# Attention heads in consecutive groups of four, tokens split by parity, and kT and qT written by VectorE's block transposes from the third group on

## The chip, the cores and the metric

The kernel runs on one core of one Trainium2 chip. The metric is device time in microseconds (us). The five engines are TensorE (PE in the profile; its weight loads are the row PEld), VectorE (DVE), ScalarE (ACT), GpSimd (POOL) and SyncE (SP). SP does no arithmetic here: it issues nearly all DMAs, in the order in which they stand in its queue.

## The reference, cut to what matters

```python
def sm_attn(qq, kk, vv):                       # softmax(qq kk^T / 8) vv
    s = scale * np.matmul(qq, kk.transpose(0, 1, 3, 2))
    a = np.exp(s - np.max(s, axis=-1, keepdims=True))
    return np.matmul(a / (np.sum(a, axis=-1, keepdims=True) + 1e-09), vv)
# q, k, v: 4 batches x 8 heads x 576 tokens x 64;  p: 4 x 8 x 32 x 64
p_packed = sm_attn(p, k, v)                    # 32 packed rows a head
x = sm_attn(q, p_packed, p_packed)             # 2304 tokens x 512 (8 heads side by side)
w = domain_probs / domain_probs.sum(-1)        # 2304 x 4
y = sum(w[:, e:e+1] * (np.maximum(x @ w1[e], 0) @ w2[e]) for e in range(4))   # 512 -> 1024 -> 512
h = y @ w_in                                   # 512 -> 2048
out = ((a0 + a1 h + a2 h^2 + a3 h^3) / (1 + |b0||h| + |b1|h^2)) @ w_out       # 2048 -> 512
```

## The kernel before

The attention is worked in eight groups of four heads (32 heads in all; two groups, x and y, for each batch bb). A group holds 4 x 32 packed rows on the 128 partitions. For each group k and q must stand with the head dimension on the partitions (tiles kT and qT: 128 partitions, 4 heads, 288 columns; partitions 0 to 63 hold one half of the tokens and 64 to 127 the other half). Both are loaded with tokens on 96 partitions, and TensorE turns them: `st_tr(i, nm, j)` (L293) makes six transposes for two heads into PSUM, and ScalarE copies them out (L294). So a group takes four calls of st_tr, two for k and two for q.

The rest of a group runs through short steps. `st_s1` multiplies p by kT (tile s), VectorE takes the maximum (mx), ScalarE the exponential (tile e). `st_e1t` transposes e on TensorE. `st_pp` multiplies by v (tile pp), VectorE scales it (ppd). `st_ppt` transposes that (tile bd). `st_s2` multiplies q by it, and VectorE transposes the scores in blocks of 32 x 32 (tile t). `st_m2`, `st_e2` and `st_a2` are the second softmax on VectorE, GpSimd and ScalarE. `st_at` turns it back in blocks, and `st_sp` splits it into a high and a low part (tiles aH and aL). `st_wb` and `st_wbl` fold the packed rows into the expert weight (tile wb).

Groups 0 and 1 run ahead of everything (the prologue, the first 28 us). The other six run between the units of the mixture of experts: 256 units (e, bb, half, c), numbered kk, each with six products into h (`emit_h`, L549), relu and split on ScalarE and VectorE (hh, hl) and, two units later, twelve products into acc (`emit_out`, L617). After them come 96 units of the last layer, with more columns each. The order in time is written out by hand: `at_step(kk, w, f, ...)` puts a step into unit kk, at w = 0 behind its h products and at w = 1 behind its acc products. The table of batch bb starts at unit s0 = (bb-1)*13 + 3 - bb//3, that is at 3, 16 and 28. All engines take their instructions in the program's order, so a waiting instruction holds back those behind it on its engine. All attention steps between the units share one PSUM buffer of two banks (`bank2`).

A group's tiles for k, q and v have one buffer each. The load of the next group is issued when the last transpose (or, for v, the last product) has read it. `store` writes rows of the output; its rows come in the token order that the loads made.

## Time and profile before

| what | value |
|---|---|
| time, median of 3 runs | 1133.42 us (1131.04 to 1133.48) |
| the profiled execution: its own time | 1133.6 us |
| its span, first to last instruction | 1131.8 us |
| PE busy | 1111.0 us, 98% |
| PEld busy | 1021.8 us, 90% |
| DVE / ACT / POOL busy | 718.9 / 522.2 / 314.0 us |
| granted TensorE clock, mean | 0.993 of full speed |
| moved by DMA | 125.93 MB |

The program stands in four stages: the prologue to 28 us, the units that have attention steps between them to some 180 us, the other units of the experts to some 700 us, and the last layer. Busy shares over the whole span mix these stages, so each is read by itself. A busy PE counts as busy while its products are in the pipeline; how far its weight loads (PEld) follow each other without a gap shows better whether it waits.

### The profile page before, as it was taken

The numbers are of one execution on the slowest core, as the hardware profiler recorded it, in microseconds if no ns is written. First come the engines' busy times: TensorE is split into PE (matmuls) and PEld (weight loads), VectorE is DVE, ScalarE is ACT, GpSimd is POOL, SyncE is SP. The second block draws the span as 40 slices with busy tenths as digits, with TensorE's granted clock in tenths as the row PEclk, the third lists the DMA queues.
The fourth block names the chain that finished last, engine by engine and source line by source line (L and its number), as shares of the span: only waits on it lengthen the run. The fifth ranks groups of instructions, "written<-read, shape, count | busy, mean of one in ns | idle before, by whom it ended". The sixth has DMA issues, their size and how long they took to land.

```text
span 1131.8 us, 20514 instructions
## 1 busy us (share of the span) xinstructions
PE 1111.0 (98%) x8145; PEld 1021.8 (90%) x8145; DVE 718.9 (64%) x1381; ACT 522.2 (46%) x1055; POOL 314.0 (28%) x315
## 2 busy tenths in 40 slices
PE   8899999999999999999999999999999999999997
PEld 6678788999999999999999999989999999999996
DVE  3343535727777746676442332599988888888885
ACT  4433433232222332222323221467778777787774
POOL 0511211132323343222433211253432222222222
PEclk9899999999999999999999999999999999999999
DMA  9542323332345233345310000533333634344421
GB/s 261 132 127 69 79 60 137 118 104 94 109 140 171 94 106 101 115 144 160 108 30 6 9 9 6 172 114 126 129 132 112 201 115 137 128 157 149 138 94 56
DMA packets 61920, 125.93 MB, mean 111 GB/s; under 512 B 6960, under 2 KB 29488, under 8 KB 61824
## 3 DMA queue, kind: packets, MB, share of 16 engines
q1 hardware_dynamic: 61504, 123.79, 35.5%
q8 instruction: 64, 1.05, 0.4%
q0 software_dynamic: 320, 0.82, 0.3%
q14 instruction: 32, 0.26, 0.1%
HBM read 103.06 MB, written 21.53 MB: 110 GB/s over the span
## 4 chain that ended last, share of the span: by engine, by line
PE 94%; DVE 2%; ACT 2%; POOL 1%; issue 1%; DMA 0%; POOLq 0%; ACTq 0%; DVEq 0%
PE acc L617 52%; PE h L549 36%; PE wb L147 3%; PE tr L293 1%; PE s L302 1%; PE e1t L327 1%; PE pp L339 0%; POOL t L378 0%; ACT e L315 0%; DVE mm L387 0%; DVE mx L310 0%; PE pT L274 0%; ACT hh L557 0%; PE pT L251 0%; DVE hl L558 0%
## 5 line engine op out<-in xcount | busy, mean ns | idle before, releaser
L617 PE MATMUL acc<-hh,w 128*128 128x288 f32 x2048 | 449.8, 296 | 0.0
L617 PEld LDWEIGHTS acc<-hh,w 128*128 128x128 f32 x2048 | 340.9, 188 | 8.8 <-issue 6.3
L558 DVE SCALAR_TENSOR_TENSOR hl<-h,hh 128x288 fp32r<-128x288 f32 x256 | 116.8, 456 | 294.0 <-ACT hh L557 293.5
L617 PE MATMUL acc<-hl,w 128*128 128x288 f32 x1024 | 300.8, 294 | 0.0
L557 ACT ACTIVATE hh<-h 128x288 fp32r<-128x288 f32 x256 | 104.9, 410 | 337.7 <-PE h L549 322.0
L549 PE MATMUL h<-aH,wb 128*128 128x288 f32 x1024 | 216.3, 300 | 2.2 <-ACT aH L405 2.2
L549 PE MATMUL h<-xH,w 128*128 128x384 f32 x768 | 196.2, 337 | 0.0
L617 PE MATMUL acc<-w,hh 128*128 128x512 f32 x576 | 193.1, 392 | 2.0 <-ACT s L563 2.0
L617 PEld LDWEIGHTS acc<-hl,w 128*128 128x128 f32 x1024 | 192.6, 188 | 0.0
L549 PEld LDWEIGHTS h<-aH,wb 128*128 128x128 f32 x1024 | 163.0, 188 | 28.6 <-issue 17.8
L594 POOL TENSOR_TENSOR hl<-c,hh 128x384 fp32r<-128x384 f32 x94 | 96.3, 1025 | 264.1 <-ACT hh L593 137.6
L549 PE MATMUL h<-aL,wb 128*128 128x288 f32 x512 | 151.3, 295 | 1.6 <-POOL aL L406 1.6
L549 PEld LDWEIGHTS h<-xH,w 128*128 128x128 f32 x768 | 140.1, 188 | 7.0
L549 PE MATMUL h<-xL,w 128*128 128x384 f32 x384 | 129.0, 336 | 0.0
L617 PEld LDWEIGHTS acc<-w,hh 128*128 128x128 f32 x576 | 108.8, 189 | 21.8 <-ACT s L563 2.3
L674 POOL TENSOR_TENSOR acc<-add,acc 128x288 f32<-128x288 f32 x96 | 75.9, 823 | 140.5 <-DVE add L672 140.5
L617 PE MATMUL acc<-w,hl 128*128 128x512 f32 x288 | 112.6, 391 | 0.0
L561 ACT ACTIVATE c<-h,small 128x384 f32<-128x384 f32 x96 | 64.7, 674 | 88.7 <-PE h L549 87.9
L549 PEld LDWEIGHTS h<-aL,wb 128*128 128x128 f32 x512 | 96.5, 188 | 2.4 <-POOL aL L406 2.4
L212 POOL TENSOR_TENSOR t<-u,raw 128x512 fp32r<-128x512 f32 x32 | 41.4, 1294 | 187.3 <-ACT raw L211 187.3
L567 DVE SCALAR_TENSOR_TENSOR m<-s,small,m 128x384 f32<-128x384 f32 x96 | 59.8, 623 | 47.9 <-ACT s L563 43.3
L549 PEld LDWEIGHTS h<-xL,w 128*128 128x128 f32 x384 | 72.2, 188 | 0.0
(111 smaller groups left out, 1291.9 us busy)
## 6 DMA issues: line engine op xcount, KB each, us to landing
w<-nw SPq DMA_DIRECT2D x96, 512.0 KB, 4.3
r<-in_moe_w_dram SPq DMA_DIRECT2D x32, 256.0 KB, 2.7
raw<-in_moe_w_in_dram SPq DMA_DIRECT2D x16, 512.0 KB, 4.3
raw<-in_moe_w_out_dram SPq DMA_DIRECT2D x16, 512.0 KB, 3.7
nw<-raw SPq DMA_DIRECT2D x32, 256.0 KB, 2.3
nw<-t SPq DMA_DIRECT2D x32, 256.0 KB, 2.6
r<-in_moe_w_dram SPq DMA_DIRECT2D x7, 1024.0 KB, 6.1
pw<-prow SPq DMA_DIRECT2D x32, 144.0 KB, 3.3
```

What stands on the lines that cost most here:

```text
L147: nc.tensor.matmul(ps[32 * c:32 * c + 32, g, :], bd[r, 2 * bb + g, 32 * c:32 * c + 32], raw1[fh][r, c, f], start=True, stop=True, tile_pos ...
L212: nc.gpsimd.tensor_tensor(out=wl, in0=f32(u), in1=f32(wh), op=ALU.subtract)
L293: nc.tensor.transpose(ps[:, hh, c * KP:c * KP + KP], src[2 * j + hh][:, c * 2 * D:(c + 1) * 2 * D], ident[:KP, :KP])
L302: nc.tensor.matmul(ps[32 * c:32 * c + 32, par, :HALF], w[r, 32 * c:32 * c + 32], xT[r, c, :], start=True, stop=True, tile_position=(64 * p ...
L549: nc.tensor.matmul(ps[:, :n], w, x, start=(i == 0), stop=(i == len(ops) - 1))
L557: nc.scalar.activation(out=hh, in_=ph, func=AF.Relu)
L558: nc.vector.scalar_tensor_tensor(out=hl, in0=ph, scalar=0.0, in1=f32(hh), op0=ALU.max, op1=ALU.subtract)
L561: nc.scalar.activation(out=c, in_=ph, func=AF.Identity, scale=a_sb[:, 3:4], bias=a_sb[:, 2:3])
L567: nc.vector.scalar_tensor_tensor(out=o, in0=x, scalar=scalar, in1=y, op0=op0, op1=op1, **kw)
L594: low.tensor_tensor(out=hl, in0=c, in1=f32(hh), op=ALU.subtract)
L617: nc.tensor.matmul(ps[:, :n], w, x, start=(first and i == 0), stop=(last and i == 2))
L674: nc.gpsimd.tensor_tensor(out=dst, in0=add, in1=dst, op=ALU.add)
```

## The change

Groups are heads 0 to 3 and 4 to 7 of a batch (before: even and odd heads). The two halves of the tokens are now the even and the odd tokens (before: by a token's place in runs of six).

Groups 0 and 1 keep their transposes on TensorE. Their loads and all loads of v have runs of 512 bytes (before 1536), so three times as many. The load of the probabilities has runs of 32 bytes (before 96). Each load of w1 is cut into two with 64 partitions each.

Groups 2 to 7 get k and q by `st_rows`: four DMAs for each tile, with 32 partitions each and runs of 128 bytes, laid out so that 32 x 32 block transposes on VectorE (`st_turn`, one for each head) give kT and qT directly. The 24 calls of st_tr for these groups and their copies on ScalarE are gone, and 48 calls of st_turn are there.

In the hand-written table the turns of k stand at s0 - 1 to s0 for group x and at s0 + 3 to s0 + 5 for group y, those of q behind s1. For x, s1 and e1t move half a unit later, m2, a2 half a unit earlier. For y, e1t moves one unit later.

```diff
-            nc.sync.dma_start(out=pn, in_=probs.rearrange("(b p c) e -> p b c e", p=KP, c=NKC))
+            nc.sync.dma_start(out=pn.rearrange("p b (j a) e -> p (b j) (a e)", a=2), in_=probs.rearrange("(b j p a) e -> p (b j) (a e)", b=B, p=KP, a=2))
...
-            nc.sync.dma_start(out=raw1[fh][:, :, f], in_=w1[e][:, fh * FH + f.start:fh * FH + f.stop].rearrange("(k p) f -> p k f", p=P))
+            src = w1[e][:, fh * FH + f.start:fh * FH + f.stop].rearrange("(g h d) f -> g d h f", g=2, d=D)
+            for g in range(2):
+                nc.sync.dma_start(out=raw1[fh][D * g:D * g + D, :, f], in_=src[g])
...
-            src = {"kr": k, "qr": q, "vr": v}[nm][i // 2].rearrange("(h g) (p c) d -> g p h (c d)", g=2, p=KP)[i % 2]
+            src = {"kr": k, "qr": q, "vr": v}[nm][i // 2].rearrange("(g h) (j p a) d -> g p (h j) (a d)", g=2, p=KP, a=2)[i % 2]
...
-            for b_ in range(2):
-                nc.scalar.copy(out=pT[:, 4 * j + 2 * b_:4 * j + 2 * b_ + 2, :].rearrange("p g (c n) -> p g c n", c=NH),
-                               in_=ps[:, 2 * b_ * P:2 * b_ * P + 2 * P].rearrange("p (c g n) -> p g c n", c=NH, g=2))
+            nc.scalar.copy(out=pT[:, 4 * j:4 * j + 4, :].rearrange("p g n -> p (g n)"), in_=ps)
...
-            if j == 1 and i > 1:
-                load(i + 1, nm)
+        LANE = 32
+        def st_rows(i, nm):
+            if i >= NIT:
+                return
+            x = ap1.tile([P, NH * NKC * D], F32, tag=nm, name=nm)[:, :NH * HALF].rearrange("p (n l) -> p n l", l=LANE)
+            st.setdefault(i, {})[nm] = x
+            src = {"kr": k, "qr": q}[nm][i // 2].rearrange("(g h) (m t a) (e l) -> g a e t (h m) l", g=2, t=LANE, a=2, l=LANE)[i % 2]
+            for g in range(4):
+                nc.sync.dma_start(out=x[LANE * g:LANE * g + LANE], in_=src[g // 2, g % 2])
+        def st_turn(i, nm, h):
+            d = st[i]
+            dst = nm[0] + "T"
+            if h == 0:
+                d[dst] = ap1.tile([P, NH, HALF], F32, tag=dst, name=dst)
+            m = HALF // LANE
+            nc.vector.transpose(out=d[dst][:, h, :], in_=d[nm][:, m * h:m * h + m].rearrange("p n l -> p (n l)"))
+            if h == NH - 1:
+                st_rows(i + 1, nm)
...
-                (0, 0, st_tr, x, "kr", 0), (0, 1, st_tr, x, "kr", 1),
-                (1, 0, st_s1, x), (2, 0, st_e1t, x),
-                (2, 1, st_tr, x, "qr", 0), (3, 0, st_tr, x, "qr", 1),
...
+                (-1, 0, st_turn, x, "kr", 0), (-1, 1, st_turn, x, "kr", 1), (0, 0, st_turn, x, "kr", 2), (0, 1, st_turn, x, "kr", 3),
+                (1, 1, st_s1, x), (1, 1, st_turn, x, "qr", 0), (2, 1, st_e1t, x), (2, 1, st_turn, x, "qr", 1),
+                (3, 0, st_turn, x, "qr", 2), (3, 0, st_turn, y, "kr", 0), (3, 1, st_pp, x), (3, 1, st_turn, x, "qr", 3),
...
-                bb, c = blk // NKC, blk % NKC
-                row = 2 * (c % NJ) + c // NJ
+                bb, half, i0 = r0 // S, r0 % S // HALF, r0 % HALF
+                n = min(HALF - i0, t0 + P - r0)
```

What stands in a row on an engine, before and now, at three places.

TensorE, unit 6, where group 2's q is turned (tr is the PSUM tile of the transposes, qr the loaded q, h and acc the units' products). Before:

```order
L617 MATMUL acc<-hh,w 128x288
L293 MATMUL tr<-ident,qr 128x96 x6
L549 MATMUL h<-aH,wb 128x288 x2
L549 MATMUL h<-aL,wb 128x288
L549 MATMUL h<-aH,wb 128x288 x2
L549 MATMUL h<-aL,wb 128x288
L293 MATMUL tr<-ident,qr 128x96 x6
L617 MATMUL acc<-hh,w 128x288
```

Now:

```order
L636 MATMUL acc<-hh,w 128x288
L348 MATMUL e1t<-ident,e_681 96x128 x6
L568 MATMUL h<-aH,wb 128x288 x2
L568 MATMUL h<-aL,wb 128x288
L568 MATMUL h<-aH,wb 128x288 x2
L568 MATMUL h<-aL,wb 128x288
L636 MATMUL acc<-hh,w 128x288
```

Both sets of six transposes are gone; e1t of group 2 has come down from the middle of unit 5 to its end.

VectorE, units 6 to 8, where group 2 reaches its second scores (hl is the units' own step, kr and qr the loaded tiles). Before:

```order
L558 SCALAR_TENSOR_TENSOR hl<-h,hh 128x288
L342 TENSOR_SCALAR ppd<-pp,rs 128x64
L558 SCALAR_TENSOR_TENSOR hl<-h,hh 128x288
L351 COPY bd<-pp 128x128
L367 STREAM_TRANSPOSE t_842<-s_833 128x288 x2
L558 SCALAR_TENSOR_TENSOR hl<-h,hh 128x288
```

Now:

```order
L577 SCALAR_TENSOR_TENSOR hl<-h,hh 128x288
L315 STREAM_TRANSPOSE qT<-qr 128x288
L315 STREAM_TRANSPOSE kT<-kr 128x288
L363 TENSOR_SCALAR ppd<-pp,rs 128x64
L315 STREAM_TRANSPOSE qT<-qr 128x288
L315 STREAM_TRANSPOSE kT<-kr 128x288
L577 SCALAR_TENSOR_TENSOR hl<-h,hh 128x288
L372 COPY bd<-pp 128x128
L315 STREAM_TRANSPOSE kT<-kr 128x288
L388 STREAM_TRANSPOSE t_835<-s_826 128x288 x2
L398 TENSOR_REDUCE mm<-t_835 128x18
L577 SCALAR_TENSOR_TENSOR hl<-h,hh 128x288
```

Five turns stand between these steps, three of them already of group 3 (kT<-kr), and the first of those stands ahead of ppd of group 2.

SP's queue, where group 3's k and q are loaded (r2 are expert weights, pw probabilities). Before:

```order
L118 DMA r2_589<-in_moe_w2_dram 128x512
L266 DMA kr_636<-in_k_dram 96x4x384
L118 DMA r2_641<-in_moe_w2_dram 128x512
L223 DMA pw_650<-prow_95 128x288
L118 DMA r2_689<-in_moe_w2_dram 128x512
L118 DMA r2_738<-in_moe_w2_dram 128x512
L266 DMA qr_759<-in_q_dram 96x4x384
L266 DMA vr_800<-in_v_dram 96x4x384
```

Now:

```order
L120 DMA r2_599<-in_moe_w2_dram 128x512
L306 DMA kr_631<-in_k_dram 32x36x32 x4
L120 DMA r2_639<-in_moe_w2_dram 128x512
L225 DMA pw_648<-prow_95 128x288
L120 DMA r2_689<-in_moe_w2_dram 128x512
L120 DMA r2_730<-in_moe_w2_dram 128x512
L268 DMA vr_785<-in_v_dram 96x12x128
L306 DMA qr_788<-in_q_dram 32x36x32 x4
```

The loads keep their places among the others, with four DMAs for one, and v now stands ahead of q.

## Rows read from the trace of the kernel before

**Rows 1.** Windows by stage: length, busy us of each engine (instructions), granted clock, DMA.

```profile
0.00:28.00 28.00, 24.29 (x325) 18.48 (x325) 10.22 (x33) 12.06 (x24) 2.50 (x8) 1.00 1.01 262
...
60.00:180.00 120.00, 115.94 (x1256) 97.74 (x1241) 53.41 (x125) 45.98 (x84) 19.93 (x17) 1.00 0.32 80
180.00:700.00 520.00, 520.00 (x4113) 496.03 (x4112) 293.59 (x593) 143.59 (x299) 151.88 (x154) 1.00 0.30 94
700.00:1117.00 417.00, 414.98 (x2172) 381.70 (x2171) 345.48 (x592) 302.48 (x612) 122.02 (x118) 1.00 0.40 129
```

**Rows 2.** The page, the chain that ended last: shares of the span by engine.

```profile
PE 94%; DVE 2%; ACT 2%; POOL 1%; issue 1%; DMA 0%; POOLq 0%; ACTq 0%; DVEq 0%
```

**Rows 3.** Timeline of weight loads, unit 6: start, us, group [idle before <- releaser].

```profile
51.78 0.19 PEld L617 LDWEIGHTS acc<-hh,w 128*128 128x128 f32 x1
51.91 0.60 PEld L293 LDWEIGHTS tr<-ident,qr 96*128 96x128 f32 x6
52.45 0.30 PEld L549 LDWEIGHTS h<-aH,wb 128*128 128x128 f32 x2
...
53.10 0.19 PEld L549 LDWEIGHTS h<-aL,wb 128*128 128x128 f32 x1
53.43 0.53 PEld L293 LDWEIGHTS tr<-ident,qr 96*128 96x128 f32 x6
53.90 0.19 PEld L617 LDWEIGHTS acc<-hh,w 128*128 128x128 f32 x1
...
55.68 0.72 PEld L339 LDWEIGHTS pp<-vr,eT 96*32 96x32 f32 x48 [0.17 <-issue]
```

**Rows 4.** The same timeline, where group 3 (a group y) waits.

```profile
65.52 0.18 PEld L302 LDWEIGHTS s<-kT,pT 64*32 64x32 f32 x16 [0.75 <-ACT kT L294]
69.22 0.61 PEld L327 LDWEIGHTS e1t<-ident,e 128*96 128x96 f32 x6 [0.64 <-ACT e L315]
```

**Rows 5.** The same timeline, group 2 (the first x) in units 4 and 5.

```profile
44.77 0.53 PEld L293 LDWEIGHTS tr<-ident,kr 96*128 96x128 f32 x6 [0.84 <-ACT kT L294]
46.24 0.18 PEld L302 LDWEIGHTS s<-kT,pT 64*32 64x32 f32 x16 [0.17 <-ACT kT L294]
46.88 0.19 PEld L617 LDWEIGHTS acc<-hh,w 128*128 128x128 f32 x1 [0.47 <-issue]
49.76 0.61 PEld L327 LDWEIGHTS e1t<-ident,e 128*96 128x96 f32 x6 [0.46 <-ACT e L315]
```

**Rows 6.** Timeline of VectorE there: group 1 is turned back behind GpSimd.

```profile
46.30 0.48 DVE L399 STREAM_TRANSPOSE aT<-t 128x288 f32<-128x288 f32 x1 [0.79 <-POOL t L390]
```

**Rows 7.** DMA: window of p's 256-byte runs (as rows 1); issues, us to landing.

```profile
2.00:2.60 0.60, 0.60 (x5) 0.60 (x4) 0.00 (x0) 0.02 (x1) 0.00 (x0) 1.00 0.83 191
...
pk<-in_p_dram SPq DMA_DIRECT2D x1, 256.0 KB, 3.3
...
kr<-in_k_dram SPq DMA_DIRECT2D x4, 576.0 KB, 4.4
```

**Rows 8.** Prologue: group 1's q issued, probabilities read, q turned; landings.

```profile
6.56 2.73 SPq L266 DMA_DIRECT2D acc<-in_q_dram  x2
...
11.79 0.25 DVE L81 TENSOR_REDUCE psm<-pn 96x24 f32<-96x96 f32 x1
...
21.82 1.02 PEld L293 LDWEIGHTS tr<-ident,acc 96*128 96x128 f32 x12 [0.17 <-issue]
...
acc<-in_q_dram SPq DMA_DIRECT2D x2, 288.0 KB, 11.2
...
pn<-in_moe_domain_probs_dram SPq DMA_DIRECT2D x1, 36.0 KB, 8.9
```

**Rows 9.** The end: GpSimd issues the last rows; stores, us to landing.

```profile
1125.29 1.10 POOL L660 DMA_DIRECT2D out_dram<-y  x2 [0.29 <-DVE y L648]
...
out_dram<-y SPq DMA_DIRECT2D x2, 192.0 KB, 3.3
out_dram<-y POOLq DMA_DIRECT2D x2, 192.0 KB, 4.4
```

More of the change, by code (lines that the diff above doesn't have):

```diff
@@ L262, in load @@
             else:
-                parts = [ap1.tile([KP, NH, NKC * D], F32, tag=nm, name=nm)]
+                parts = [ap1.tile([P, NH * NKC * D], F32, tag=nm, name=nm)[:KP].rearrange("p (h x) -> p h x", h=NH)]
             n = NH // len(parts)
             for j, tl in enumerate(parts):
-                nc.sync.dma_start(out=tl, in_=src[:, j * n:j * n + n])
+                nc.sync.dma_start(out=tl.rearrange("p h (j x) -> p (h j) x", j=NJ), in_=src[:, j * n * NJ:(j + 1) * n * NJ])
             d[nm] = [tl[:, h] for tl in parts for h in range(n)]
@@ L452 @@
         load_pw(0)
-        for nm in ("kr", "qr", "vr"):
-            load(2, nm)
+        load(2, "vr")
+        for nm in ("kr", "qr"):
+            st_rows(2, nm)
         st_a2(0)
@@ L496 @@
             for s, w, f, *args in (
-                (0, 0, st_tr, x, "kr", 0), (0, 1, st_tr, x, "kr", 1),
-                (1, 0, st_s1, x), (2, 0, st_e1t, x),
-                (2, 1, st_tr, x, "qr", 0), (3, 0, st_tr, x, "qr", 1),
-                (3, 1, st_pp, x), (4, 0, st_ppt, x), (4, 1, st_s2, x),
-                (5, 0, st_m2, x), (5, 0, st_tr, y, "kr", 0),
-                (5, 1, st_e2, x), (5, 1, st_tr, y, "kr", 1),
-                (6, 0, st_a2, x), (6, 0, st_s1, y),
-                (7, 0, st_e1t, y), (7, 1, st_at, x), (7, 1, st_tr, y, "qr", 0),
-                (8, 0, st_sp, x), (8, 0, st_tr, y, "qr", 1),
-                (8, 1, st_pp, y), (9, 0, st_ppt, y), (9, 1, st_s2, y),
-                (10, 0, st_m2, y), (10, 0, st_wb, 0, bb, 0), (10, 1, st_wbl), (10, 1, st_e2, y),
-                (11, 0, st_a2, y), (11, 0, st_wb, 0, bb, 1), (11, 1, st_wbl), (11, 1, st_at, y),
-                (12, 0, st_sp, y),
+                (-1, 0, st_turn, x, "kr", 0), (-1, 1, st_turn, x, "kr", 1), (0, 0, st_turn, x, "kr", 2), (0, 1, st_turn, x, "kr", 3),
+                (1, 1, st_s1, x), (1, 1, st_turn, x, "qr", 0), (2, 1, st_e1t, x), (2, 1, st_turn, x, "qr", 1),
+                (3, 0, st_turn, x, "qr", 2), (3, 0, st_turn, y, "kr", 0), (3, 1, st_pp, x), (3, 1, st_turn, x, "qr", 3),
+                (3, 1, st_turn, y, "kr", 1), (4, 0, st_ppt, x), (4, 0, st_turn, y, "kr", 2), (4, 1, st_s2, x),
+                (4, 1, st_m2, x), (5, 0, st_turn, y, "kr", 3), (5, 1, st_e2, x), (5, 1, st_a2, x),
+                (6, 0, st_s1, y), (6, 1, st_turn, y, "qr", 0), (7, 0, st_turn, y, "qr", 1), (7, 1, st_at, x),
+                (8, 0, st_e1t, y), (8, 0, st_sp, x), (8, 0, st_turn, y, "qr", 2), (8, 1, st_pp, y),
+                (8, 1, st_turn, y, "qr", 3), (9, 0, st_ppt, y), (9, 1, st_s2, y), (10, 0, st_m2, y),
+                (10, 0, st_wb, 0, bb, 0), (10, 0, st_e2, y), (10, 1, st_wbl), (11, 0, st_wb, 0, bb, 1),
+                (11, 1, st_a2, y), (11, 1, st_wbl), (11, 1, st_at, y), (12, 0, st_sp, y),
             ):
@@ L653, in store @@
             while r0 < t0 + P:
-                blk, i0 = r0 // KP, r0 % KP
-                n = min(KP - i0, t0 + P - r0)
-                bb, c = blk // NKC, blk % NKC
-                row = 2 * (c % NJ) + c // NJ
+                bb, half, i0 = r0 // S, r0 % S // HALF, r0 % HALF
+                n = min(HALF - i0, t0 + P - r0)
                 queue = nc.gpsimd if u[1] == NPAIR - 1 and r0 > t0 else nc.sync
-                queue.dma_start(out=out[bb * S:(bb + 1) * S, :].rearrange("(p c) f -> c p f", c=NKC)[row, i0:i0 + n, :], in_=y[r0 - t0:r0 - t0 + n, :])
+                queue.dma_start(out=out[bb * S:(bb + 1) * S, :].rearrange("(n a) f -> a n f", a=2)[half, i0:i0 + n, :], in_=y[r0 - t0:r0 - t0 + n, :])
                 r0 += n
```

## The prediction

> **What bounds the kernel now.** I read first the windows by stage, then the chain that ended last, then the weight loads of the attention stage one by one. TensorE is the busiest engine in every stage, but the stages differ [rows 1]: from 180 to 700 us it is busy for all of the time, from 700 to 1117 for 415 of 417, and in the attention stage, 60 to 180 us, for 115.9 of 120. There the weight loads, which show gaps better, fill 97.7 us. The granted clock is 1.00 (the level of 2.4 GHz) in all of these rows. The chain runs through PE for 94% [rows 2]. So behind the prologue, work taken off TensorE shortens the run by its own length, as long as no other engine is late in its place; and what the attention stage gains is passed on whole, since the later stages wait for nothing else. The prologue is another matter: the DMA engines are at 1.01 of their capacity through its 28 us [rows 1], and the reader is to see in it how near each load lands to its use.
>
> **What goes: the transposes on TensorE.** In unit 6 the sixth set's first weight load starts at 51.91 and the next h at 52.45: 0.54 us. The other set lies between an h at 53.10 and an acc at 53.90; neighbours without it start 0.13 apart (51.78 to 51.91), so it costs 0.80 - 0.13 = 0.67 [rows 3]. The mean is 0.60 us for a call of st_tr. 24 calls go. The two for group 2's k lie in a place that TensorE does not bound (below), so 22 x 0.60 = 13.2 us.
>
> Waits go with them. In group 3 the scores wait 0.75 us for ScalarE's copy of kT, and its e1t 0.64 us for the exponential [rows 4]; groups 5 and 7 repeat both within 0.01. A wait of 0.17 is left for a copy that came in time [rows 5], so 3 x (0.75 - 0.17) = 1.7. The second goes because e1t of y now stands two units behind its s1 and not one: 3 x 0.64 = 1.9. Together 3.6 us.
>
> Group 2 alone is different. Its turns share VectorE with the end of group 1. VectorE starts group 1's aT at 46.30, after GpSimd [rows 6], ends it at 46.78, and the last turn of k stands behind it: it ends at 46.78 + 0.48 = 47.3. Scores cannot start before that. From there TensorE does s and the bubble behind it (46.24 to 46.88, 0.64 with the 0.47 in it [rows 5]), one unit of 18 products at 520 us / 4113 = 0.126, so 2.3 [rows 1], and e1t, 0.6, with some 0.2 for changes between them: the end of unit 5 comes at about 51.1, against 51.91 before. That is 0.8 us, though two sets and waits of 0.84 and 0.46 [rows 5] go.
>
> **What comes: 48 turns on VectorE.** One turn of 128 x 288 between SBUF tiles took 0.48 us [rows 6]: 48 x 0.48 = 23.0 us. VectorE is busy for 53.4 us of 60 to 180 [rows 1]; some 40 of the 48 fall there, 19.2, which makes 72.6 of 120, or 61%. The cover is that share and the two units by which acc follows hl. What would be late if the cover were gone: behind a turn stand hl, ppd, bd and the maximum mx, for which TensorE waits soonest. The bounds are 0 and one turn ahead of two of these in each of six groups, 12 x 0.48 = 5.8 us. In the order the turns stand behind ppd and mx as a rule, so I take 0.7.
>
> The Trainium skill (VectorE: DVE Perf Modes, Rules for kernel authors) advises TensorE for a 128 x 128 transpose where PSUM may be the destination. Per tile the trace agrees that TensorE is cheaper, 0.60 us for two heads [rows 3] against 2 x 0.48 [rows 6]; but that compares engines of which one has no time left, and by the rule the sum would keep TensorE's 13.2 us.
>
> **What comes: loads in runs of 128 bytes.** k or q of a group is 576 KB, 4608 runs now where one load had 384, and that landed after 4.4 us [rows 7]. No row shows 128-byte runs in this size. The nearest is p, 256-byte runs, which moved at 191 GB/s alone and landed after 3.3 us; 256 KB at that rate are 1.4 us, so 1.9 are fixed [rows 7]. If the bytes set the rate, 576 KB take 3.1 us; if the packets do, twice that, 6.2. So a load lands after 5.0 to 8.1 us. I take 6.
>
> Who waits: the first turn of y's k stands on VectorE ahead of x's ppd. In the first batch the load is issued at 47.3; TensorE wants ppd after s, two units, e1t, pp and an h: 47.3 + 0.6 + 2 x 2.3 + 0.6 [rows 5] + 0.7 [rows 3] + 0.8 (six products), and 1.0 as an estimate for the gaps between kinds: 55.6. A turn and ppd, with their semaphores, take about 1.3 of it. So 7.0 us are free. In the two other batches s stands a unit further behind the last turn: about 9. For q, three units pass until the turn and hl gives two more: about 11, with v's load ahead of it on SP. At 6 us all three fit; at 8.1 the first batch loses 1.1. On SP nothing queued behind is wanted soon: the weight r2 behind the four issues serves a unit three steps on. I take 0 and keep 0 to 1.1.
>
> **Prologue.** Loads keep their bytes but have runs of 512 for 1536, and the probabilities 32 for 96. The probabilities take 8.9 us to land and are read at 11.79 [rows 8]; no row here shows slack, so I count none, though VectorE has more than a microsecond free behind. Group 1's q lands last of what is timed here: its second half is issued by 6.56 + 2.73 = 9.3, some 9.0 at its start, lands 11.2 later, at 20.2, and is used at 21.82 [rows 8]: 1.6 us of slack. If only bytes count, nothing changes. If 512-byte runs moved no faster than p's, 191 for 262 GB/s [rows 1, 7], the 3.7 MB to that point would take 19.4 for 14.1 us: 5.3 later, less the slack, 3.7. I take 1.0, nearer to the low end since 512 is nearer to the larger runs in cost per byte. Two halves of a w1 load add issues only; the one ACT copy of pT for two is worth nothing here.
>
> **End.** The last rows leave in two parts, the second by GpSimd, issued at 1125.29 and later, 4.4 us to landing, against 3.3 on SP [rows 9]. Now the last two blocks go whole on SP: between 0 and 1.3 less; I take 0.8.
>
> **Sum.** 13.2 + 3.6 + 0.8 - 0.7 - 0 - 1.0 + 0.8 = 16.7 us. The profiled execution took 1133.6 us, its span 1131.8: 1133.6 - 16.7 = 1116.9 us. The median of before is 1133.42, 0.2 lower, which I leave aside; 0.3%, 3.4 us, is about what a measurement of this kernel can tell from no change.
>
> **Rivals.**
> *VectorE and the prologue take more.* For it: in unit 6 five turns stand in a row with other steps. Against it: 61% busy and two units of lag. At the bounds the sum is 13.2 + 3.6 + 0.8 - 5.8 - 1.1 - 3.7 = 7.0, so 1126.6; the case covers 1121 to 1127.
> *The 128-byte loads are late.* Then VectorE waits for a load ahead of ppd, and TensorE behind it. Let a load take R us. Lost are (R - 7) + 2 (R - 9) + 3 (R - 11) = 6 R - 58, which eats 16.7 at R = 12.5: from there the kernel is slower. For it: no row has such runs. Against it: a 128-byte packet would have to take longer than one of 256, at whose packet rate R is 8.1. If it took twice as long, R is 2 x 6.2 + 1.9 = 14.3, the loss 27.8 and the time 1133.6 - 16.7 + 27.8 = 1144.7.
> The Trainium skill (DMA: Bandwidth & Descriptors, Specifications) says that below 512 bytes the engine reads and writes again what it transfers, and that line rate needs 512. The trace agrees in part: p's 256-byte runs reached 191 GB/s [rows 7], less than the prologue's 262 [rows 1], not half of it. By the rule a short run would cost about twice, an estimate that gives the 14.3 and 1144.7 above.
> *The change does not bring what it says.* TensorE's freed time turns into waits for hh and hl, because the chain through ScalarE and VectorE is as long: 1130 to 1137. Against it: the idle time of TensorE in 60 to 180 is 4 us in all [rows 1], and ScalarE loses 24 copies.
> *More is gained.* The waits in front of acc shrink too, and the prologue costs nothing: under 1112.
>
> **How the numbers follow.** The forecast, 1112 to 1121, has 60%. VectorE and prologue, 1121 to 1127, 22%. Late loads 10%: 7 with R over 12.5 and a time above 1137, 3 with a load between 9 and 12 and a time still under 1130. No gain 4%. More gain 4%. Faster by over 0.3%: 0.60 + 0.22 + 0.03 + 0.04 = 0.89; within: 0.04; slower: 0.07. The range 1111 to 1126 leaves out the late loads, the case without gain and the edges of two others, about 2 in 10.
>
> **What would show it.** Right: no transposes of k and q behind the prologue, TensorE's busy time some 14 us lower, the 180 us mark of before at about 164, turns near 0.48 us, loads of k and q near 6 us, the granted clock still 1.00. VectorE's case would show as waits of TensorE for ppd, bd or hl; the loads' as VectorE idle before a turn, ended by a DMA; the prologue's as a first h later than before by over 2 us. I am wrong if the loads take over 9 us, or if TensorE's idle time in the attention stage grows by more than 5.

## The result, and the profile of the changed kernel

The changed kernel took 1122.72 us (median of five runs, 1122.08 to 1124.24), the kernel before 1132.83 beside it: a ratio of 0.9914, with a 95% interval of 0.9900 to 0.9929. That is 10.1 us less. The forecast was 1116.9, 16.7 us less, so the time lies inside its range and on its side, but past 1121, where its likeliest case ended: four tenths of the gain did not arrive. The profiled execution took 1124.24 us, its span 1122.5; the span before was 1131.8.

The windows by stage, in the columns of [rows 1], for the changed kernel:

```profile
0.00:28.00 28.00, 23.70 (x269) 17.77 (x271) 6.93 (x25) 10.16 (x19) 1.34 (x7) 0.80 1.02 190
...
60.00:180.00 120.00, 118.78 (x1288) 101.74 (x1287) 75.31 (x180) 39.85 (x75) 25.23 (x21) 1.00 0.68 103
...
700.00:1117.00 417.00, 414.55 (x2153) 379.85 (x2151) 348.06 (x601) 305.12 (x617) 123.98 (x120) 1.00 0.40 131
```

The attention stage did what was forecast: TensorE is idle there for 1.2 of 120 us instead of 4, and VectorE's 75.3 us are the 63% that the forecast put at 61. The first row is the bad one: the granted clock fell from 1.00 to 0.80 and the loads from 262 to 190 GB/s. The chain that ended last has a new member, SP's own queue, which did not stand in [rows 2] at all:

```profile
PE 93%; SPq 3%; DMA 1%; DVE 1%; POOL 1%; ACT 0%; issue 0%; POOLq 0%; ACTq 0%
```

Where the 9.3 us of span lie is read from a step that stands at the same unit in both kernels: the VectorE half of wb, in unit 13 and again when the attention is over. Before (start, us, engine line):

```profile
83.13 1.23 DVE L136 TENSOR_TENSOR wb<-wb 128x1024 fp32r<-128x1024 f32 x1 [0.69 <-ACT wb L149]
...
176.23 1.22 DVE L136 TENSOR_TENSOR wb<-wb 128x1024 fp32r<-128x1024 f32 x1 [0.69 <-ACT wb L149]
```

and in the changed kernel:

```profile
88.14 1.23 DVE L138 TENSOR_TENSOR wb<-wb 128x1024 fp32r<-128x1024 f32 x1 [0.69 <-ACT wb L151]
...
169.28 1.22 DVE L138 TENSOR_TENSOR wb<-wb 128x1024 fp32r<-128x1024 f32 x1 [0.69 <-ACT wb L151]
```

Up to unit 13 the changed kernel is 5.0 us **behind**, although the transposes of groups 2 and 3 are gone by then. Between the two marks it needs 81.1 us for 93.1 and gains 12.0. What is left, from 176.23 and 169.28 to the ends of the spans, is 955.6 against 953.2: 2.4 less. The question for the experiments is what was lost ahead of unit 13.

**The lead.** SP issues every load, one after the other. This is its queue around the end of the prologue in the kernel before (start, us, what is issued):

```profile
22.96 0.38 SPq L266 DMA_DIRECT2D kr<-in_k_dram  x1
23.43 0.43 SPq L266 DMA_DIRECT2D qr<-in_q_dram  x1
23.91 1.01 SPq L266 DMA_DIRECT2D vr<-in_v_dram  x1
34.15 0.35 SPq L118 DMA_DIRECT2D r<-in_moe_w_dram  x1
```

and in the changed kernel:

```profile
2.87 1.93 SPq L268 DMA_DIRECT2D vr<-in_v_dram  x1
4.85 2.69 SPq L76 DMA_DIRECT2D pn<-in_moe_domain_probs_dram  x1
7.58 2.16 SPq L77 DMA_DIRECT2D small<-in_moe_a_dram  x1
...
10.26 0.43 SPq L268 DMA_DIRECT2D qr<-in_q_dram  x1
...
28.69 14.34 SPq L306 DMA_DIRECT2D kr<-in_k_dram  x4
43.13 3.13 SPq L306 DMA_DIRECT2D qr<-in_q_dram  x4
46.36 1.90 SPq L120 DMA_DIRECT2D r<-in_moe_w_dram  x3
```

Before, SP was through with group 2 at 24.92 and then idle for 9 us, until the buffer for the next expert weight r came free at 34.15. Now the four issues of group 2's k last 14.34 us where one lasted 0.38, those of q 3.13, and r goes out at 46.36. Who waits is seen on ScalarE, which copies each r into w. Before, the fourth of these copies, and in the changed kernel the same copy and the hh behind it:

```profile
43.28 0.61 ACT L124 ACTIVATE w<-r 128x512 fp32r<-128x512 f32 x1
```

```profile
51.26 0.63 ACT L126 ACTIVATE w<-r 128x512 fp32r<-128x512 f32 x1 [3.10 <-DMA r<-in_moe_w_dram]
51.79 0.39 ACT L576 ACTIVATE hh<-h 128x288 fp32r<-128x288 f32 x1
```

Behind hh stand hl on VectorE, behind hl the turns of k, and behind these TensorE's scores of group 2 (VectorE first, then the weight loads):

```profile
52.22 0.46 DVE L577 SCALAR_TENSOR_TENSOR hl<-h,hh 128x288 fp32r<-128x288 f32 x1 [4.55 <-ACT hh L576]
...
53.42 0.42 DVE L315 STREAM_TRANSPOSE kT<-kr 128x288 f32<-128x288 f32 x1
```

```profile
53.90 0.13 PEld L323 LDWEIGHTS s<-kT,pT 64*32 64x32 f32 x2 [3.12 <-DVE kT L315]
...
56.31 0.50 PEld L568 LDWEIGHTS h<-aH,wb 128*128 128x128 f32 x2 [0.92 <-issue]
```

The rows name VectorE's kT as what the scores waited for. But k itself had long landed (at 45.6; its first two turns were done by 47.7); the wait began at a weight of the MoE that stood in SP's queue behind loads it has nothing to do with.

**Theory.** SP is held while it issues loads of many short runs, in the prologue and for group 2; what stands behind them is late, and the fourth weight r sets when unit 5 can go on. **Rivals:** the short runs cost by their rate alone; the low clock is the cost; VectorE's turns or the new places in the order cost more than forecast; w1, which now loads in two halves of 64 partitions, fills the DMA engines for longer. The first is hard to part from the theory, since the engines are full while SP is held: their share from 36 to 43 us is 1.09, and was 0.22 before. The last was not tried, as no run puts w1 back; its rows stand with the prologue's term below.

### The profile page after: what moved, and what is told of

Read it like the earlier page. It is cut to its first block, busy times and chain, and to the rows that moved or that the text cites. A ratio compares the mean times of both kernels' runs of the same rounds, so it can differ in the third digit from the quotient of the medians.

```text
span 1122.5 us, 20286 instructions
## 1 busy us (share of the span) xinstructions
PE 1103.7 (98%) x8001; PEld 1013.9 (90%) x8001; DVE 737.1 (66%) x1429; ACT 508.4 (45%) x1029; POOL 312.9 (28%) x311
## 4 chain that ended last, share of the span: by engine, by line
PE 93%; SPq 3%; DMA 1%; DVE 1%; POOL 1%; ACT 0%; issue 0%; POOLq 0%; ACTq 0%
PE acc L636 53%; PE h L568 36%; PE wb L149 3%; SPq L306 2%; DMA r<-in_moe_w_dram 1%; SPq L268 1%; PE s L323 1%; PE pp L360 0%; PE e1t L348 0%; SPq L76 0%; SPq L115 0%; PE pp L276 0%; SPq L77 0%; POOL t L411 0%; DVE mm L408 0%
```

## The experiments

The table has every run that was timed, with the median and the ratio to the kernel before on the same chip, and from its profile the start of the first h, the granted clock of 0 to 28 us, the start of the fourth w copy and of wb in unit 13 (all us). The changed kernel stands twice, the second time beside short_filled, small_q2 and best2. The kernel before took 1131.9 us beside short_loads, small_q, best1 and runs_q, and 1132.8 to 1132.9 beside the others, so a comparison across these goes by the ratios. First h, clock and the last two columns are each of one profile.

| kernel | time | ratio (95%) | first h | clock | 4th w | unit 13 |
|---|---|---|---|---|---|---|
| before | 1132.8 | 1 | 28.8 | 1.00 | 43.3 | 83.1 |
| changed | 1122.7 | 0.9914 (0.9900–0.9929) | 33.5 | 0.80 | 51.3 | 88.1 |
| changed again | 1123.0 | 0.9919 (0.9902–0.9937) | 32.8 | 0.87 | 50.3 | 86.5 |
| old_runs | 1120.3 | 0.9890 (0.9874–0.9907) | 28.9 | 1.00 | 47.8 | 83.6 |
| q_late | 1118.3 | 0.9871 (0.9856–0.9885) | 35.3 | 0.86 | 47.2 | 82.1 |
| g2_tensor | 1124.0 | 0.9916 (0.9893–0.9938) | 30.6 | 0.94 | 48.8 | 87.5 |
| turns_twice | 1124.2 | 0.9926 (0.9909–0.9943) | 29.1 | 1.00 | 49.4 | 85.3 |
| short_loads | 1137.3 | 1.0053 (1.0040–1.0066) | 30.9 | 0.88 | 47.5 | 89.8 |
| short_filled | 1138.2 | 1.0051 (1.0035–1.0066) | 30.2 | 1.00 | 47.4 | 89.6 |
| small_q | 1117.0 | 0.9872 (0.9858–0.9886) | 36.8 | 0.95 | 46.1 | 80.5 |
| small_q2 | 1116.3 | 0.9857 (0.9842–0.9872) | 29.8 | 0.94 | 42.9 | 78.1 |
| best1 | 1119.0 | 0.9890 (0.9877–0.9903) | 30.0 | 1.00 | 44.5 | 83.1 |
| best2 | 1116.2 | 0.9857 (0.9840–0.9874) | 28.0 | 1.00 | 43.8 | 79.6 |
| runs_q | 1114.6 | 0.9847 (0.9833–0.9860) | 28.8 | 1.00 | 43.3 | 77.7 |

### Batch 0 in its old, longer runs (old_runs)

```diff
+            if i < 2:
+                src = {"kr": k, "qr": q, "vr": v}[nm][0].rearrange("(g h) (p c) d -> g p h (c d)", g=2, p=KP)[i]
...
-            nc.sync.dma_start(out=pn.rearrange("p b (j a) e -> p (b j) (a e)", a=2), in_=probs.rearrange("(b j p a) e -> p (b j) (a e)", b=B, p=KP, a=2))
+            nc.sync.dma_start(out=pn[:, 0], in_=probs[:S].rearrange("(p c) e -> p c e", c=NKC))
+            nc.sync.dma_start(out=pn[:, 1:].rearrange("p b (j a) e -> p (b j) (a e)", a=2), in_=probs[S:].rearrange("(b j p a) e -> p (b j) (a e)", b=B - 1, p=KP, a=2))
```

> The changed kernel, but batch 0 (groups 0 and 1) keeps the old token order: its k, q, v rows load in runs of 1536 bytes, its probabilities in runs of 96, and its result rows go out in the old order. Everything else is the changed kernel. Theory (the prologue's loads are slower in short runs and hold SP's queue, and all behind it is late): the window 0:28 goes back to a clock of 1.00 and about 260 GB/s, the first h starts near 29 instead of 33.5, group 2's rows are issued from about 23 to 24 instead of 28.7, r2 lands earlier; the time is 1114 to 1118 us, ratio 0.983 to 0.987. Rival (the early loss is in the new places of the table and VectorE's turns of group 2): first h near 29 all the same, but the gain is lost again by unit 6, h of unit 6 starts near 61 and the time stays at 1121 to 1124.

Measured: 1120.3 us. The first h came at 28.88 with the clock at 1.00, as the theory said, 4.7 us ahead of the changed kernel's profile. That is no proof that the longer runs did it: turns_twice below has the changed kernel's prologue, and shows 29.1 and 1.00 as well. And the time fell by 2.4 only; its weight loads and then ScalarE show why:

```profile
28.88 0.42 PEld L575 LDWEIGHTS h<-aH,wb 128*128 128x128 f32 x2 [1.02 <-ACT aH L433]
```

```profile
47.84 0.63 ACT L127 ACTIVATE w<-r 128x512 fp32r<-128x512 f32 x1 [4.49 <-DMA r<-in_moe_w_dram]
```

TensorE starts early and then waits longer: SP is through with group 2 at 42.8 instead of 46.3, the fourth copy is 3.4 us earlier, and the spans differ by 3.7 (1118.8 for 1122.5). The prologue and the weight are not two costs; the later of the two counts, and it is the weight. turns_twice says the same: with its first h at 29.1, GpSimd is done with the buffer of r at 34.5, but r goes out at 45.1 and is copied at 49.4.

### Group 2's q out of the weight's way (q_late)

```diff
-        for nm in ("kr", "qr"):
-            st_rows(2, nm)
+        st_rows(2, "kr")
...
-                               (3, 1, st_at, 1, 1), (4, 0, st_sp, 1, 1)):
+                               (3, 1, st_at, 1, 1), (4, 0, st_sp, 1, 1), (2, 0, st_rows, 2, "qr")):
```

> The changed kernel, but the four 128-byte-run loads of group 2's q leave their place ahead of the expert weights of unit 3 and are issued in unit 2 instead. Theory (r2, queued on SP behind group 2's loads, comes late, ScalarE waits 3.1 us for it at 51.3, and hh, hl, the turns of kT and s behind it): first h unchanged at 33.5; r2 is issued near 43 instead of 46.4, ScalarE's wait for it falls below 1 us, s of group 2's wait for kT from 4.3 below 2; 1119 to 1121 us, ratio 0.988 to 0.990. Rival (k's rows themselves land too late, or VectorE is too slow at turning them): s of group 2 still ends near 56 and the time is 1122 to 1124.

Measured: 1118.3 us, 4.4 less, and more than the theory asked for. The queue, and the weight loads at the first h and behind group 2's scores:

```profile
41.87 3.62 SPq L120 DMA_DIRECT2D r<-in_moe_w_dram  x3
45.59 3.73 SPq L306 DMA_DIRECT2D qr<-in_q_dram  x4
```

```profile
35.28 0.30 PEld L567 LDWEIGHTS h<-aH,wb 128*128 128x128 f32 x2
...
51.77 0.30 PEld L567 LDWEIGHTS h<-aH,wb 128*128 128x128 f32 x2 [0.46 <-issue]
```

This profile has the later first h of the two, 35.28 against the changed kernel's 33.54, and is still 6.3 us shorter in span. No other step was taken away; the place of one load in SP's queue made the difference. The k rows' landing as the limit has fallen with it. Part of the 6.3 us is the clock: from 34 to 60 us it is granted at 1.00 here, while in the changed kernel it falls behind the wait (see the sum at the end).

### Group 2 on TensorE (g2_tensor)

```diff
+                if f is st_turn and args[0] == 2:
+                    if args[2] > 1:
+                        continue
+                    f = st_tr
+                    s, w = ((0, args[2]) if args[1] == "kr" else ((2, 1), (3, 0))[args[2]])
                 at_step(s0 + s, w, f, *args)
```

> The changed kernel, but group 2 alone loads k and q as groups 0 and 1 do (runs of 512 bytes) and is turned by TensorE in four sets, k's in unit 3, q's in units 5 and 6; its other steps stay at their new places, groups 3 to 7 are as changed. Theory (the 128-byte loads in the prologue hold the queue): SP is through with group 2's loads by 33 instead of 46, ScalarE's wait for r2 is gone, s of group 2 waits for kT under 1 us; minus 4 of waits, plus 2.4 for four sets of 0.6 us: 1119 to 1122 us, ratio 0.988 to 0.991. Rival (the queue holds nothing that matters, VectorE's turns are free): four sets more and nothing gained, 1124 to 1126.

Measured: 1124.0 us, the rival's number, but not for its reason. Runs of 512 bytes hold SP too: group 2's three loads were issued from 26.8 to 38.2, r at 38.26, and ScalarE still waited. ScalarE, then TensorE behind it:

```profile
48.75 0.63 ACT L126 ACTIVATE w<-r 128x512 fp32r<-128x512 f32 x1 [3.61 <-DMA r<-in_moe_w_dram]
```

```profile
50.26 0.60 PEld L293 LDWEIGHTS tr<-ident,kr 96*128 96x128 f32 x6 [4.56 <-ACT kT L294]
```

So 2.5 us of the lateness went and four sets of transposes came. The 128-byte runs alone are not the cause. Nor is the issue alone: this r landed 10.5 us after 38.26, with the DMA engines at a share of 1.18 from 38 to 48 us.

### Each turn of groups 3 to 7 twice (turns_twice)

```diff
-            nc.vector.transpose(out=d[dst][:, h, :], in_=d[nm][:, m * h:m * h + m].rearrange("p n l -> p (n l)"))
+            for _ in range(1 + (i > 2)):
+                nc.vector.transpose(out=d[dst][:, h, :], in_=d[nm][:, m * h:m * h + m].rearrange("p n l -> p (n l)"))
```

> The changed kernel, but every VectorE turn of groups 3 to 7 is made twice, the second time onto the first: 40 turns of 0.47 us more on VectorE, 19 us. It prices the turns where the loads are in time. Theory (VectorE has room there, the turns are free as forecast): 1122 to 1125 us, ratio 0.990 to 0.993. Rival (VectorE is the bound while the groups run, and part of the missing gain is its time): a good part of the 19 us shows, 1128 to 1140, with more waits of s for kT and qT and of h for a free bank (hl late).

Measured: 1124.2 us, 1.1 to 1.4 more, with 40 turns and 19 us more on VectorE. Between the marks of unit 13 and the end of the attention, where 32 of them lie, it needs 81.9 us against 81.1:

```profile
85.28 1.23 DVE L138 TENSOR_TENSOR wb<-wb 128x1024 fp32r<-128x1024 f32 x1 [0.69 <-ACT wb L151]
...
167.14 1.23 DVE L138 TENSOR_TENSOR wb<-wb 128x1024 fp32r<-128x1024 f32 x1 [0.69 <-ACT wb L151]
```

VectorE as the bound has fallen: a second set of turns costs 0.7 us there, so the first cannot have cost many. (No run prices the first set itself.)

### The kernel before with the shorter runs (short_loads)

Here the table of steps and the transposes of before stand in the changed kernel's code, and all loads of k, q and v come in runs of 512 bytes, the probabilities in runs of 32. The halves of w1 stay in it too, so it does not price the runs alone:

```diff
-            src = {"kr": k, "qr": q, "vr": v}[nm][i // 2].rearrange("(h g) (p c) d -> g p h (c d)", g=2, p=KP)[i % 2]
+            src = {"kr": k, "qr": q, "vr": v}[nm][i // 2].rearrange("(g h) (j p a) d -> g p (h j) (a d)", g=2, p=KP, a=2)[i % 2]
```

> The kernel before with the changed order of heads and tokens: groups of four heads in a row, tokens by parity, so that every k, q and v load comes in runs of 512 bytes and the probabilities in runs of 32; all transposes stay on TensorE at their old places, and no 128-byte run is loaded. It prices the shorter runs alone, in a kernel where nothing later waits for the loads behind them. Theory (the eight small pieces queued behind k and v come 2 us later, pp of group 0 waits about 2 us for eT, which waits for b; where the granted clock then falls, sets and copies of the prologue take twice as long): between plus 0.3 us (first h near 29, clock 1.00) and plus 6 (first h near 34, clock 0.8), from run to run: median 1133 to 1138, ratio 1.000 to 1.005, and 0:28 at about 190 to 200 GB/s. Rival (the new order is only a matter of the table and of VectorE): 1132.8, ratio 1.000 within 0.001, first h at 28.8.

Measured: 1137.3 us, 5.4 more than before, an interval of 0.4 to 0.66% that leaves out the rival. The theory's time held; its reason, the clock, is tried next. SP here, and ScalarE:

```profile
30.97 5.81 SPq L268 DMA_DIRECT2D vr<-in_v_dram  x1
36.87 12.97 SPq L120 DMA_DIRECT2D r<-in_moe_w_dram  x4
```

```profile
47.50 0.63 ACT L126 ACTIVATE w<-r 128x512 fp32r<-128x512 f32 x1 [1.84 <-DMA r<-in_moe_w_dram]
```

### The same with TensorE kept busy in its wait (short_filled)

```diff
         st_s1(1)
+        warm[0] = 16
         st_pp(0)
```

> The kernel before with the shorter runs (the run of that name before it), and 16 transposes of the identity to no use on TensorE ahead of pp of group 0, 1.7 us of work in the 2 us in which it waits for eT. It prices the fall of the clock alone: the wait stays, the loads stay as late. Theory (of the 5.4 us that the shorter runs cost there, most is the low clock behind that wait): the clock holds 1.00 to 28, tr of q takes 1.08 us and not 2.04, 1133 to 1135, ratio 1.001 to 1.003. Rival (the cost is the loads' rate, and that the weights and group 2's loads stand behind them): no better than 1136.5.

Measured: 1138.2 us, and the theory as written has fallen. The granted clock did what was meant: in the same stretch the changed kernel, then this one:

```profile
20.00:24.00 4.00, 4.00 (x57) 2.25 (x59) 0.66 (x2) 1.57 (x3) 0.00 (x0) 0.50 1.17 225
```

```profile
20.00:24.00 4.00, 3.19 (x77) 2.00 (x78) 1.72 (x5) 0.89 (x2) 0.00 (x0) 1.00 1.15 237
```

0.50 is the level of 1.2 GHz and 1.00 that of 2.4; TensorE had waited 2.35 us for eT ahead of the fall in the changed kernel. Without the fall nothing was gained, since the fourth copy is where it was:

```profile
47.43 0.63 ACT L126 ACTIVATE w<-r 128x512 fp32r<-128x512 f32 x1 [3.45 <-DMA r<-in_moe_w_dram]
```

ScalarE waits 3.45 instead of 1.84. In these kernels (ratios 1.0053 and 1.0051) the low clock of the prologue costs nothing, as the time is set elsewhere.

### The small loads behind the large ones (small_q, small_q2)

Both keep the changed kernel's short runs and its order of tokens, with q as in q_late. The probabilities, a and b load behind the first two groups:

```diff
-        load_small()
         load(0, "qr")
         load(1, "vr")
         load(1, "qr")
+        load_small()
```

In small_q the work on the probabilities follows the prologue's last step, in small_q2 it is in units 1 to 3:

```diff
-        for s, w, f, *args in ((0, 0, st_wb, 0, 0, 0, FB), (0, 1, st_wbl), (1, 0, put_w2, 0, 1), (1, 1, st_wb, 0, 0, 1),
+        for s, w, f, *args in ((1, 0, prep_small), (2, 0, prep_rows), (3, 0, load_pw, 0), (0, 0, st_wb, 0, 0, 0, FB), (0, 1, st_wbl), (1, 0, put_w2, 0, 1), (1, 1, st_wb, 0, 0, 1),
```

> The changed kernel in its own order of tokens and its short runs, with q of group 2 in unit 2, and the probabilities, a and b loaded behind all of the first two groups' k, q and v, with the work on them behind the prologue. Theory (the short runs do harm only by what they make late: b, and through it eT of group 0; the clock falls in the 2 us that TensorE then waits): pp of group 0 waits under 1 us for eT, the clock stays at 1.00 to 28, first h at 28.5 to 29.5, 1115.5 to 1117.5, ratio 0.984 to 0.986, nearly as with the longer runs. Rival (the rate itself is the cost): first h still at 31 or more, and 1118 to 1119 as with q later alone.

Measured: 1117.0. pp of group 0 waited 0.51 us for eT, as the theory said, but my edit put a new wait in: TensorE stood 6.4 us for the transpose of the probabilities, so neither first h nor clock came out, and the run does not decide.

```profile
PE pnT L97 <- DVE small L90: 6.4, 1, 6.4
```

> The run with the small loads behind the first two groups' and q of group 2 in unit 2, but with the work on the probabilities in units 1 to 3, so that TensorE doesn't wait in the prologue for its transpose (it did, 6.4 us). Theory (the short runs do harm by what they make late, b first): clock 1.00 to 28, first h near 28, k of group 2 issued from 26 at the latest, s of group 2 done by 48 to 49; 1114 to 1116, as with the longer runs. Rival (the rate itself is the cost): 1117 or more.

Measured: 1116.3 us. That lies between the two expected cases, nearer to the theory, 2.0 less than q_late and 6.4 less than the changed kernel, with runs of 512 bytes as before. What settles it is best2 below, which has the same edits and batch 0's longer runs: 1116.2 beside this 1116.3. With the small loads out of the way the short runs of batch 0 cost nothing that can be seen. The rate shows part of the reason. From 10 to 14 us, in the kernel before, in the changed one and in small_q2 (the last number is GB/s, the one ahead of it the DMA share):

```profile
10.00:14.00 4.00, 3.34 (x46) 2.21 (x48) 2.31 (x13) 2.11 (x7) 0.00 (x0) 1.00 1.13 231
```

```profile
10.00:14.00 4.00, 3.35 (x48) 2.11 (x36) 2.38 (x13) 1.90 (x4) 0.00 (x0) 1.00 0.73 105
```

```profile
10.00:14.00 4.00, 3.35 (x78) 2.28 (x79) 1.44 (x5) 2.58 (x5) 0.00 (x0) 1.00 1.23 215
```

In the changed kernel there is a hole: from 4.85 to 9.74 SP was held at the probabilities and a, so that q could be issued at 10.26 only, and the DMA engines ran dry. With q issued ahead of them the same runs move at 215. In small_q2 the hole comes later (141 and 161 GB/s from 16 to 24 us), where less waits for it.

### Both edits together, and two tries at more (runs_q, best1, best2)

runs_q has the edits of old_runs and q_late and nothing else.

> Two of the edits together: batch 0 in the old order and runs of 1536 bytes, and group 2's q issued in unit 2. Theory (what counts is when the expert weights of unit 3 land, and so when SP is through with group 2's k: 46.4 in the changed kernel, 42.9 with the longer runs, 41.9 with q later; with both near 39.5): s of group 2 ends 2 to 3 us earlier than with q later alone, 1115 to 1117, ratio 0.984 to 0.986. Rival (the two gains add in full, each a cost of its own): minus 2.4 and minus 4.4 from 1122.7, 1115.9; and if the gains are the same thing twice, 1118 as with q later alone.

Measured: 1114.6 us, 8.2 less than the changed kernel, or 7.6 by the ratios, which is the sum of the two gains (2.7 and 4.9 by the ratios). So the rival's full sum came out as well as the theory's time, and the run does not part them. Both edits shorten one queue, and there too the gains add: r goes out at 42.90 in old_runs, at 41.87 in q_late and at 38.51 here, for 46.36. The kernel beats both kernels, and the fourth copy waits for nothing:

```profile
43.31 0.62 ACT L127 ACTIVATE w<-r 128x512 fp32r<-128x512 f32 x1
```

```profile
77.66 1.23 DVE L139 TENSOR_TENSOR wb<-wb 128x1024 fp32r<-128x1024 f32 x1 [0.69 <-ACT wb L152]
```

43.31 is the time of before, 43.28, within 0.03. With it unit 13 is 5.5 us ahead of before, where the changed kernel was 5.0 behind.

best1 against runs_q:

```diff
         st_e2(0)
+        put_w2(0, 0)
         load_pw(0)
-        load(2, "vr")
         st_rows(2, "kr")
...
-                               (3, 1, st_at, 1, 1), (4, 0, st_sp, 1, 1), (2, 0, st_rows, 2, "qr")):
+                               (3, 1, st_at, 1, 1), (4, 0, st_sp, 1, 1), (2, 0, load, 2, "vr"), (2, 0, st_rows, 2, "qr")):
```

> The last one, and beside it the weights of unit 3 loaded ahead of group 2's k (their buffer is set free by an earlier put_w2), v and q of group 2 issued in unit 2. Theory (SP's queue was the bound of the first units): ScalarE's wait for r2 is gone, s of group 2 waits only for its own turns, h of the unit behind it near 46 to 48 instead of 56.3; as the changed kernel takes 1066 from there to the end, 1112 to 1115.5, ratio 0.982 to 0.985. Rival (something else, such as k's rows landing or VectorE's turns, ends last there): no better than 1116 to 1118.

Measured: 1119.0, worse. Its waits from 28 to 64:

```profile
PEld pp L283 <- DVE ppd L370: 2.9, 1, 2.9
...
DVE qT L322 <- DMA qr<-in_q_dram: 2.6, 1, 2.6
```

q landed too late, and TensorE waited for the ppd behind its turn: the forecast's rival of late loads, made by hand. VectorE also waited 3.2 us for k, and ScalarE 4.8 for later weights.

best2 is runs_q with the two edits of small_q2 on the small loads.

> Batch 0 in the old order and its longer runs, q of group 2 in unit 2, and the work on the probabilities in units 1 to 3, with their load behind the first two groups'. Against the run without the last edit (1114.6) group 2's k need no longer stand behind the wait for prow at 25.3 and can be issued from 22.5. Theory (from there on TensorE itself is the chain: s waited only 1.5 us in all): 1112.5 to 1114.5, ratio 0.9825 to 0.985. Rival (SP's queue still sets it): 3 us less, 1111 to 1112.

Measured: 1116.2, no better than runs_q (0.9857 against 0.9847, the intervals overlap), and neither case came true. The fourth copy, at 43.77, waits for nothing here either, so an earlier place in the queue has nothing left to give. Its profile reaches unit 13 at 79.6 for 77.7: TensorE waits 2.4 us at 41.1 for the work on the probabilities.

### The changed kernel again (after_again)

> The changed kernel itself, beside these runs on one chip. Both theories: 1122 to 1124, ratio 0.990 to 0.993; first h anywhere between 29 and 35 with the clock of 0:28 between 1.00 and 0.8, while h behind group 2's s starts near 54.5 to 56.5 all the same, since r2 lands no sooner.

Measured: 1123.0 us, with the first h at 32.83, the clock at 0.87 and the wait for the weight in place:

```profile
50.25 0.63 ACT L126 ACTIVATE w<-r 128x512 fp32r<-128x512 f32 x1 [5.41 <-DMA r<-in_moe_w_dram]
```

## Why the prediction was right, and where it was not

**The transposes and the waits: right.** For groups 4 to 7, 16 of the 22 sets, the forecast's terms make 16 x 0.60 = 9.6 and two thirds of 3.6, 2.4, less a part of the turns, some 0.5: 11.5 us. Between the two marks 12.0 were gained. In runs_q the same stretch is 81.1 us too. TensorE's busy time was to fall by some 14 us. It fell by 7.3 (1103.7 for 1111.0), as products at the low clock take longer; in runs_q, where the clock fell less, it is 1097.0, 14.0 less.

**The turns: right.** One takes 0.45 to 0.47 us against the forecast's 0.48 (VectorE's groups by form, mean ns):

```profile
L315 DVE STREAM_TRANSPOSE qT<-qr 128x288 f32<-128x288 f32 x24 | 11.2, 468 | 0.1
L315 DVE STREAM_TRANSPOSE kT<-kr 128x288 f32<-128x288 f32 x24 | 10.5, 449 | 0.0
```

and doubling them cost 0.7 us between the marks and 1.1 to 1.4 in all, on the side of the 0.7 that was taken, far from the bound of 5.8.

**The 128-byte loads: right that nobody waits for them, wrong in their time and in what stood behind them.** From 60 us on no step waits for a load of k or q, as forecast, but this was close. From group 3 on a load of k took 5.9 to 8.0 us from first issue to last landing and one of q 8.7 to 10.0, where 6 was taken, and the q of groups 3, 5 and 7 landed 0.2 to 0.6 us ahead of its first turn. The sign "over 9 us" came true for three loads of q, and for group 2's k with 17.0. The step that failed is the sentence "On SP nothing queued behind is wanted soon: the weight r2 behind the four issues serves a unit three steps on." Three things were wrong in it. I took an issue to be free, as the 0.3 to 0.6 us of the profile made it look, while the landing took the 6 us; the four issues of group 2's k took 14.34. I checked the queue for groups 3 and on, not for group 2's own loads at the end of the prologue. And I looked at who waits for k and q only, not at the 9 us that SP had been idle ahead of r at 34.15: that idle time was the cover, and the change used it up. r went out 12.2 us later, at 46.36. Some 4.8 of this is the late prologue of this profile (GpSimd is done with the buffer at 38.9, before at 34.1), the other 7.5 the queue. "Who waits" was then ScalarE, at the head of the chain that feeds VectorE's turns and TensorE's scores.

**Group 2 early, plus 0.8: wrong through the same wait.** Its scores were forecast for 47.3 and the last of them started at 55.18. In runs_q, with the queue mended, they started from 45.5 to 47.3, and unit 5 ended at 50.9, where 51.1 was forecast.

**The prologue, minus 1.0: wrong in size and in kind.** The shorter runs and w1 in halves cost 5.4 us together in the kernel before (short_loads), more than my bound of 3.7, and the changed kernel regains 2.4 with batch 0's longer runs (old_runs). The bound came from a rate, 191 GB/s, that the prologue then happened to show, by luck: it is not the rate of 512-byte runs. From 6 to 10 us these moved at 236 against 250. The Trainium skill (DMA: Bandwidth & Descriptors, Specifications) gives 512 bytes as the least for line rate, and the trace agrees but for these 6%. Of the 2.0 MB that 190 for 262 GB/s leave unmoved in 28 us, 0.5 are the hole from 10 to 14, and 1.3 are missing from 16 to 28. There a second step failed: "Two halves of a w1 load add issues only". In the kernel before and in runs_q, whose first two groups load in the same long runs, nearly all that moves from 20 to 24 us is expert weights, at a full share of the engines:

```profile
20.00:24.00 4.00, 3.30 (x80) 2.23 (x81) 2.79 (x6) 1.38 (x3) 0.00 (x0) 1.00 1.07 377
```

```profile
20.00:24.00 4.00, 3.30 (x83) 2.19 (x80) 2.79 (x6) 1.34 (x3) 0.00 (x0) 1.00 1.12 212
```

At these rates the 2 MB of the first w1 take 5.6 and 9.9 us, an estimate, and group 2's loads and r stand behind them. What differs in these loads is the halves of 64 partitions; but no run puts them back, so their part of the lost time is not shown.

**The end, plus 0.8: right.** From TensorE's last product to the end of the span it was 7.2 us and is 6.3. Of the stores of the last 11 us GpSimd issues two, where it issued six; its last one goes out as early as TensorE ends and not behind it, as in [rows 9]:

```profile
1116.12 0.53 POOL L677 DMA_DIRECT2D out_dram<-y  x1 [0.78 <-ACT y L669]
```

The other 1.4 of the 2.4 us behind the marks lie between the last stage's first h and its last product: 406.3 us before, 404.8 changed. I don't count them, because the other kernels, whose code is the same there, show both lengths (406.4 in runs_q, 404.8 in q_late). It is the clock: where that stage is long, TensorE is granted 0.50 for some 3 us some 20 us into it (738 to 741 us before, 721 to 724 in runs_q), and 1.00 all through in the changed kernel and in q_late; in all 14 profiles the two go together. So 1.4 of the 9.3 us of span are luck of the profiles.

**The sum.** With a fourth copy at 51.26 instead of some 43.3 the changed kernel lost 8.0 us; the forecast had taken 1.0 for the prologue and hoped for 0.8 from group 2. Of the 10.5 us by which runs_q is ahead at unit 13 (77.66 for 88.14), some 2 more are the clock. Behind the wait the changed kernel's next unit, from h to e1t, takes 4.3 us at a granted clock of 0.50, and in runs_q 2.35 at 1.00:

```profile
60.59 0.83 PEld L348 LDWEIGHTS e1t<-ident,e 128*96 128x96 f32 x6
```

```profile
47.88 0.30 PEld L574 LDWEIGHTS h<-aH,wb 128*128 128x128 f32 x2 [0.46 <-issue]
...
50.23 0.69 PEld L355 LDWEIGHTS e1t<-ident,e 128*96 128x96 f32 x6
```

Where the weight is on time again, runs_q takes 1114.6, 2.3 below the forecast. So the mechanism and the terms of the steady part stand, and the missing 5.8 us come from one wait and the fall of the clock behind it. The rival that came true in time, 1121 to 1127, was named for VectorE and the prologue. Its sign for the prologue, a first h more than 2 us later, came true (33.5 for 28.8), but the time was lost through SP's queue and ScalarE, in loads of the prologue and of group 2. What is left open: why an issue is held. That the queue takes only so many pieces at a time fits the runs here (the same four issues took 2.6 to 5.4 us for the later k, and 5.1 to 6.4 for the later q, which stands behind v), but no row shows the queue's fill. Open too is how much of it is w1's halves.

## What to carry to other kernels

A load is not only a landing time: ask how long its issue can hold the queue when its runs become short, and what stands behind it, for whichever engine. Idle time of a DMA queue's issuer ahead of a load that waits for its buffer is cover, and should be priced like any other before it is spent. Late starts do not add up: find the one that ends last (here a weight, not the first h or the low clock of the prologue), because only that one pays when mended. A load cut into halves of fewer partitions is not only more issues: compare its rate. Small loads that nobody wants soon can go behind large ones that somebody does; this gained 2.0 us with the short runs (small_q2 against q_late) and nothing with the long ones (best2).
